# Crossbar DMA transposes for q, k and the attention output, wider score blocks and a fixed order on all engines, in a fused attention and MoE kernel

## The chip, the cores and the metric

The kernel runs on one core of a Trainium2 chip. The metric is the device time of one execution in microseconds (us), smaller is better. The profile is one execution of the same program. The engines are called PE (matmuls; PEld is its loading of weights, which overlaps PE), DVE (VectorE), ACT (ScalarE), POOL (GpSimd) and SP (SyncE, which here does nothing but issue DMAs). A "q" behind an engine's name (SPq) means its instruction queue.

## The reference

Eight batches of sliding-window attention with ALiBi bias come first; the result, 4608 tokens of 512 values, goes through one MoE-like block with a hard-swish. Cut to what matters:

```python
B, H, S, D = 8, 8, 576, 64
scores = q @ k.T / sqrt(D) + alibi_bias        # only where 0 <= i - j < 128
attn   = softmax(scores)                        # per head
x      = (attn @ v) -> [B * S, H * D] = [4608, 512]
h      = x @ w_in                               # w_in  [512, 2048]
g      = h * clip(h + 3, 0, 6) / 6
out    = g @ w_out                              # w_out [2048, 512]
```

## The kernel before

One PE stream holds everything. The attention goes by head pairs g (four pairs per batch, 32 in all); between its pieces the function `fill` puts MoE steps (four matmuls of 128x512 each), so that PE has work while the other engines do the softmax. There are 288 such steps, 144 up (`hps`) and 144 down (`ops`). An up step may be placed only when the tokens it needs have passed through attention.

The scores contract over the head dimension, so q and k are needed transposed. So does the first MoE matmul with the attention output. Before, PE makes all three transposes by matmuls with an identity, and DVE copies each result out of PSUM:

```python
def transposes(g):                       # q and k of one head pair
    b, hp = divmod(g, NP)
    for src, nm in ((qbuf[b % 2], "qT"), (kbuf[b % 2], "kT")):
        tp = ps_tp.tile([128, SP], BF16, tag="tp", name="tp")
        for j in range(NQ):              # NQ = 5
            nc.tensor.transpose(tp[:, ts(j, 128)], src[:, j, ts(hp, 128)], ident)
        t = qkt.tile([128, SP], BF16, tag=nm, name=nm)
        nc.vector.tensor_copy(out=t, in_=tp)
        st[g, nm] = t

def back(g):                             # attention output of one head pair
    avs = st[g, "avs"]
    tp = ps_tp.tile([128, SP], BF16, tag="tp", name="tp")
    for j in range(NQ):
        nc.tensor.transpose(tp[:, ts(j, 128)],
                            avs[:, j, :, :].rearrange("p e d -> p (e d)"), ident)
    nc.vector.tensor_copy(out=xT[:, hp, ds(b * S, S)], in_=tp[:, 0:S])
    done[0] = g + 1
```

The main loop fixes the order of PE alone; the other engines are ordered by the scheduler:

```python
with tc.manual_schedule(engines={mybir.EngineType.PE}):
    prepare(0)
    transposes(0)
    for g in range(G + 1):
        if g < G:
            scores_diag(g)
        if g + 1 < G:
            prepare(g + 1)               # casts; loads of the next batch
        fill(2)
        if g > 0:
            values(g - 1, (0, 1, 2))     # ends in the division result avs
        fill(1)
        if g > 0:
            values(g - 1, (3, 4))
        fill(1)
        if g < G:
            scores_off(g)
        fill(1)
        if g + 1 < G:
            transposes(g + 1)
        fill(1)
        if g > 0:
            back(g - 1)
        fill(2)
    fill(len(units))
```

The softmax here doesn't subtract the row's maximum and nothing guards it: scores larger than these inputs give would overflow.

Of the kernel before, what the change touches and what calls it, by code (L numbers as in the profile page):

```python
# [18 lines left out]
def kernel(  # L19
# [17 lines left out]
    NQ = 5  # L37
    LAST = S - 4 * 128
    SP = NQ * 128
    W = D + 1  # L40
    slopes = [2.0 ** (-8.0 * (h + 1) / H) for h in range(H)]
# [3 lines left out]
    n_nt = Ntok // NT  # L45

# [5 lines left out]
    bias3 = perm.tile([128, 1], FP32)  # L52
    rel_i = perm.tile([128, 1], INT32)
# [4 lines left out]
    loads = ctx.enter_context(tc.tile_pool(name="loads", bufs=4))  # L58
    held = ctx.enter_context(tc.tile_pool(name="held", bufs=1))
    qkt = ctx.enter_context(tc.tile_pool(name="qkt", bufs=3))  # L60
    ppool = ctx.enter_context(tc.tile_pool(name="ppool", bufs=3))
    small = ctx.enter_context(tc.tile_pool(name="small", bufs=4))
# [3 lines left out]
    ps_sc = ctx.enter_context(tc.tile_pool(name="ps_sc", bufs=1, space=bass.MemoryType.PSUM))  # L66
    ps_av = ctx.enter_context(tc.tile_pool(name="ps_av", bufs=1, space=bass.MemoryType.PSUM))
    ps_tp = ctx.enter_context(tc.tile_pool(name="ps_tp", bufs=2, space=bass.MemoryType.PSUM))
# [3 lines left out]
    qbuf = [held.tile([128, NQ, H * D], BF16, name=f"qbuf{i}") for i in range(2)]  # L72
    kbuf = [held.tile([128, NQ, H * D], BF16, name=f"kbuf{i}") for i in range(2)]
    vbuf = [held.tile([128, NQ, H, W], BF16, name=f"vbuf{i}") for i in range(2)]
    p4buf = [held.tile([128, 2, 128], BF16, name=f"p4buf{i}") for i in range(2)]

    srcs = (("qf", q), ("kf", k), ("vf", v))

    def new_loads():
        return {nm: loads.tile([128, NQ, H, D], FP32, tag="ld", name=nm) for nm, _ in srcs}  # L80

    def load_pair(got, b, hp):
        for nm, src in srcs:
            for h in (2 * hp, 2 * hp + 1):
                nc.sync.dma_start(out=got[nm][:, 0:4, h, :],
                                  in_=src[b, h, 0:512, :].rearrange("(t p) d -> p t d", p=128))
                nc.sync.dma_start(out=got[nm][:LAST, 4, h, :], in_=src[b, h, 512:S, :])  # L87

    def load_all(got, b):
        for nm, src in srcs:  # L90
            for j in range(NQ):
                n = min(128, S - j * 128)
                nc.sync.dma_start(
                    out=got[nm][:n, j, :, :],
                    in_=src[b, :, ds(j * 128, n), :].rearrange("h p d -> p h d"))

    got0 = new_loads()
    for hp in range(NP):
        load_pair(got0, 0, hp)

    make_identity(nc, ident)
    nc.vector.memset(bias3, 0.5)
    nc.gpsimd.iota(rel_i, pattern=[[0, 1]], base=0, channel_multiplier=1)
    nc.vector.tensor_copy(out=rel_f, in_=rel_i)
    for h in range(H):
        nc.vector.tensor_scalar(out=bias_d[:, h:h + 1], in0=rel_f, scalar1=-64.0,
                                scalar2=slopes[h], op0=ALU.add, op1=ALU.mult)
        nc.vector.tensor_scalar(out=bias_o[:, h:h + 1], in0=rel_f, scalar1=-192.0,
                                scalar2=slopes[h], op0=ALU.add, op1=ALU.mult)
    for i in range(2):  # L110
        nc.vector.memset(vbuf[i][:, :, :, D:W], 1.0)
        nc.vector.memset(vbuf[i][64:128, 4, :, 0:D], 0.0)
        nc.vector.memset(qbuf[i][64:128, 4, :], 0.0)
        nc.vector.memset(kbuf[i][64:128, 4, :], 0.0)
        nc.vector.memset(p4buf[i], 1.0)
# [13 lines left out]
    def cast_pair(got, b, hp, eng):  # L129
        for nm, dst in (("qf", qbuf[b % 2]), ("kf", kbuf[b % 2])):  # L130
            s = got[nm].rearrange("p j h d -> p j (h d)")
            eng.tensor_copy(out=dst[:, 0:4, ts(hp, 128)], in_=s[:, 0:4, ts(hp, 128)])  # L132
            eng.tensor_copy(out=dst[:LAST, 4, ts(hp, 128)], in_=s[:LAST, 4, ts(hp, 128)])
        hs = slice(2 * hp, 2 * hp + 2)
        vb = vbuf[b % 2]
        eng.tensor_copy(out=vb[:, 0:4, hs, 0:D], in_=got["vf"][:, 0:4, hs, :])
        eng.tensor_copy(out=vb[:LAST, 4, hs, 0:D], in_=got["vf"][:LAST, 4, hs, :])

    def cast_all(got, b):
        for nm, dst in (("qf", qbuf[b % 2]), ("kf", kbuf[b % 2])):  # L140
            s = got[nm].rearrange("p j h d -> p j (h d)")
            nc.gpsimd.tensor_copy(out=dst[:, 0:4, :], in_=s[:, 0:4, :])
            nc.gpsimd.tensor_copy(out=dst[:LAST, 4, :], in_=s[:LAST, 4, :])
        vb = vbuf[b % 2]
        nc.gpsimd.tensor_copy(out=vb[:, 0:4, :, 0:D].rearrange("p j h d -> p (j h) d"),
                              in_=got["vf"][:, 0:4, :, :].rearrange("p j h d -> p (j h) d"))
        nc.gpsimd.tensor_copy(out=vb[:LAST, 4, :, 0:D], in_=got["vf"][:LAST, 4, :, :])

    st = {}

    def transposes(g):
        b, hp = divmod(g, NP)
        for src, nm in ((qbuf[b % 2], "qT"), (kbuf[b % 2], "kT")):
            tp = ps_tp.tile([128, SP], BF16, tag="tp", name="tp")
            for j in range(NQ):
                nc.tensor.transpose(tp[:, ts(j, 128)], src[:, j, ts(hp, 128)], ident)  # L156
            t = qkt.tile([128, SP], BF16, tag=nm, name=nm)
            nc.vector.tensor_copy(out=t, in_=tp)  # L158
            st[g, nm] = t

    def scores_diag(g):
        b, hp = divmod(g, NP)
        qT, kT = st[g, "qT"], st[g, "kT"]
        sc = ps_sc.tile([128, 2, 512], FP32, tag="sc", name="sc")
        for j in range(4):
            for e in range(2):
                r = slice(e * D, (e + 1) * D)
                nc.tensor.matmul(sc[:, e, ts(j, 128)], lhsT=kT[r, ts(j, 128)],  # L168
                                 rhs=qT[r, ts(j, 128)], start=True, stop=True)
        pd = ppool.tile([128, 2, 4, 128], BF16, tag="pd", name="pd")  # L170
        for e in range(2):
            h = 2 * hp + e
            nc.scalar.activation(out=pd[:, e, :, :].rearrange("p j c -> p (j c)"),  # L173
                                 in_=sc[:, e, :], func=ACT.Exp,
                                 bias=bias_d[:, h:h + 1], scale=scale)
            nc.gpsimd.affine_select(out=pd[:, e, :, :], in_=pd[:, e, :, :],  # L176
                                    pattern=[[0, 4], [1, 128]], channel_multiplier=-1, base=0,
                                    compare_op=ALU.is_ge, fill=0.0)
        st[g, "pd"] = pd

    def scores_off(g):
        b, hp = divmod(g, NP)
        qT, kT = st[g, "qT"], st[g, "kT"]
        sc = ps_sc.tile([128, 2, 512], FP32, tag="sc", name="sc")
        for j in range(4):
            n = 128 if j < 3 else LAST
            for e in range(2):
                r = slice(e * D, (e + 1) * D)
                nc.tensor.matmul(sc[:, e, ds(j * 128, n)], lhsT=kT[r, ts(j, 128)],  # L189
                                 rhs=qT[r, ds((j + 1) * 128, n)], start=True, stop=True)  # L190
        for e in range(2):
            r = slice(e * D, (e + 1) * D)
            nc.tensor.matmul(sc[:, e, 448:512], lhsT=kT[r, 512:640],  # L193
                             rhs=qT[r, 512:576], start=True, stop=True)
        po = ppool.tile([128, 2, 4, 128], BF16, tag="po", name="po")
        p4 = p4buf[g % 2]
        for e in range(2):
            h = 2 * hp + e
            nc.scalar.activation(out=po[:, e, :, :].rearrange("p j c -> p (j c)"),  # L199
                                 in_=sc[:, e, :], func=ACT.Exp,  # L200
                                 bias=bias_o[:, h:h + 1], scale=scale)
            nc.scalar.activation(out=p4[:, e, 0:64], in_=sc[:, e, 448:512], func=ACT.Exp,  # L202
                                 bias=bias_d[:, h:h + 1], scale=scale)
            nc.gpsimd.affine_select(out=po[:, e, :, :], in_=po[:, e, :, :],  # L204
                                    pattern=[[0, 4], [-1, 128]], channel_multiplier=1, base=-1,
                                    compare_op=ALU.is_ge, fill=0.0)
        nc.gpsimd.affine_select(out=p4[:, :, 0:64], in_=p4[:, :, 0:64],
                                pattern=[[0, 2], [1, 64]], channel_multiplier=-1, base=0,
                                compare_op=ALU.is_ge, fill=0.0)
        st[g, "po"] = po  # L210
# [23 lines left out]

    def back(g):
        b, hp = divmod(g, NP)
        avs = st[g, "avs"]
# [61 lines left out]
    def prepare(g):  # L299
        b, hp = divmod(g, NP)  # L300
        if b == 0:
            cast_pair(got[0], 0, hp, nc.vector)
            if hp == 1:
                load_weights_in()
# [63 lines left out]
```

## Time and profile before

| | before |
|---|---|
| median of 3 runs | 419.31 us (417.61 to 419.33) |
| span of the profiled run | 417.7 us |
| PE busy | 81% |
| PE busy from 100 to 400 us | 93% |
| one head pair in the steady stretch | about 10 us |

The first page of the profile, kernel before: the busy time of each engine, then the span in 40 slices of 10.4 us (each digit is the busy share in tenths; PEclk is the granted PE clock in tenths), and the chain of waits that ended last ("issue" is time in which an engine waited for nothing that the profile shows).

```profile
PE 338.9 (81%) x2739; PEld 175.2 (42%) x2784; DVE 201.5 (48%) x438; ACT 198.5 (48%) x355; POOL 145.1 (35%) x217
...
PE   0141618878999899989998999899899999999985
...
PEclk9999999998999999999999999999999999999999
DMA  8989799997157989898470000001000000101011
...
PE 46%; DVE 15%; ACT 14%; issue 11%; DMA 8%; SPq 4%; POOL 1%; DVEq 0%; POOLq 0%; ACTq 0%
```

The PE row shows a start of about ten slices with many gaps, and then a stretch that is full. The windows view of the same kernel puts numbers on the two parts; its columns are the window, its length, the busy time and instruction count of PE, PEld, DVE, ACT and POOL, the granted clock, the DMA share and GB/s.

```profile
0.00:100.00 100.00, 47.72 (x492) 30.12 (x496) 44.10 (x125) 35.88 (x67) 45.15 (x69) 0.98 1.08 183
100.00:400.00 300.00, 279.55 (x2203) 140.21 (x2239) 156.06 (x312) 161.44 (x286) 99.90 (x148) 1.00 0.34 77
...
45.00:69.00 24.00, 11.61 (x130) 8.62 (x129) 8.94 (x24) 7.55 (x16) 12.00 (x17) 1.00 1.24 193
```

PE is busy 280 of 300 us after the start, so what PE has to do there sets the time. One pair of the steady stretch, in the timeline of PE (start, length, engine, line, operation, tiles; in brackets the idle time before it and what ended that):

```profile
143.17 0.40 PE L168 MATMUL sc<-qT,kT 64*128 64x128 bf16 x8
...
146.93 0.20 PE L222 MATMUL av<-vbuf,po 128*128 128x65 bf16 x1 [0.36 <-DVE avs L231]
...
149.34 0.44 PE L156 MATMUL tp<-ident,qbuf 128*128 128x128 bf16 x5
149.62 0.44 PE L156 MATMUL tp<-ident,kbuf 128*128 128x128 bf16 x5
...
150.77 0.44 PE L240 MATMUL tp<-ident,avs 128*128 128x128 bf16 x5
...
152.87 0.34 PE L168 MATMUL sc<-qT,kT 64*128 64x128 bf16 x6
```

The pair lasts from 143.17 to 152.87 us. Fifteen of its matmuls are transposes, 0.28 us for each group of five (149.34 to 149.62). Removing them, and the short wait for the division result `avs`, is what the change is after.

### The profile page before, as it was taken

Reading aid. Unit: us, or ns where it says so; the run is one execution under the profiler, and the core shown is the slowest. Engines: PE = TensorE matmul, PEld = TensorE weight load, DVE = VectorE, ACT = ScalarE, POOL = GpSimd, SP = SyncE. Lnnn points to the kernel's source line nnn. Section 1 sums busy time; section 2 is a strip of 40 time slices with the busy share of each in tenths; the row PEclk is TensorE's granted clock in tenths of the full one; section 3 lists DMA queues with packets and bytes.
Section 4 is the critical chain, followed back from the end, with each engine's and each line's share of the span. In section 5 each row is a group of like instructions: output and inputs, shape, how many; then the busy total and the mean of one; then the engine's idle time right before and its main releaser. Section 6 shows DMA issues by size and latency. Waiting matters only on the chain.

```text
span 417.7 us, 7115 instructions
## 1 busy us (share of the span) xinstructions
PE 338.9 (81%) x2739; PEld 175.2 (42%) x2784; DVE 201.5 (48%) x438; ACT 198.5 (48%) x355; POOL 145.1 (35%) x217
## 2 busy tenths in 40 slices
PE   0141618878999899989998999899899999999985
PEld 0021415445444444444454444444444444444432
DVE  3341614675455555555555555555555454344400
ACT  0240414675655565555565655556565534443400
POOL 3070464458657427342752374222222200000000
PEclk9999999998999999999999999999999999999999
DMA  8989799997157989898470000001000000101011
GB/s 134 195 148 199 151 198 197 209 201 135 49 132 166 179 176 166 161 186 152 116 163 25 27 26 27 27 27 39 32 31 27 27 25 30 48 25 52 25 70 55
DMA packets 122481, 42.40 MB, mean 101 GB/s; under 512 B 113744, under 2 KB 117840, under 8 KB 122448
## 3 DMA queue, kind: packets, MB, share of 16 engines
q1 hardware_dynamic: 118224, 37.76, 44.3%
q0 software_dynamic: 4224, 4.19, 6.2%
q8 instruction: 21, 0.34, 0.4%
q14 instruction: 12, 0.10, 0.1%
HBM read 36.70 MB, written 9.44 MB: 110 GB/s over the span
## 4 chain that ended last, share of the span: by engine, by line
PE 46%; DVE 15%; ACT 14%; issue 11%; DMA 8%; SPq 4%; POOL 1%; DVEq 0%; POOLq 0%; ACTq 0%
PE ops L267 22%; PE hps L253 13%; ACT r L257 8%; DMA vf<-in_v_dram 6%; DVE g L258 5%; DVE avs L231 4%; DVE osb L274 3%; ACT pd L173 3%; PE tp L156 2%; PE sc L168 2%; PE av L222 2%; PE sc L189 2%; ACT p4buf L202 2%; SPq L87 2%; DMA kf<-in_k_dram 2%
## 5 line engine op out<-in xcount | busy, mean ns | idle before, releaser
L258 DVE SCALAR_TENSOR_TENSOR g<-r,hps 128x512 bf16<-128x512 f32 x144 | 99.0, 687 | 117.0 <-ACT r L257 116.9
L253 PE MATMUL hps<-xT,w_in_sb 128*128 128x512 bf16 x535 | 144.4, 382 | 10.5 <-DVE xT L242 5.3
L267 PE MATMUL ops<-w_out_sb,g 128*128 128x512 bf16 x572 | 145.2, 379 | 5.6 <-DVE osb L274 3.1
L257 ACT ACTIVATE r<-hps,bias 128x512 f32<-128x512 f32 x144 | 99.2, 691 | 96.8 <-PE hps L253 93.9
L267 PEld LDWEIGHTS <-g 128*128 128x128 bf16 x576 | 53.6, 98 | 70.0 <-issue 15.1
L176 POOL TENSOR_SCALAR_AFFINE_SELECT pd<-pd 128x512 bf16<-128x512 bf16 x64 | 39.8, 644 | 96.9 <-ACT pd L173 96.9
L253 PEld LDWEIGHTS <-w_in_sb 128*128 128x128 bf16 x576 | 49.8, 98 | 49.9 <-issue 4.1
L204 POOL TENSOR_SCALAR_AFFINE_SELECT po<-po 128x512 bf16<-128x512 bf16 x64 | 40.4, 634 | 79.0 <-ACT po L199 75.7
L199 ACT ACTIVATE po<-sc,bias_o 128x512 bf16<-128x512 f32 x64 | 44.0, 687 | 39.3 <-PE sc L193 39.3
L173 ACT ACTIVATE pd<-sc,bias_d 128x512 bf16<-128x512 f32 x64 | 40.5, 683 | 43.1 <-PE sc L168 43.1
L222 PE MATMUL av<-vbuf,po 128*128 128x65 bf16 x256 | 26.1, 201 | 15.4 <-DVE avs L231 15.3
L158 DVE COPY qT<-tp 128x640 bf16<-128x640 bf16 x32 | 15.7, 492 | 35.9 <-PE tp L156 35.8
L156 PE MATMUL tp<-ident,kbuf 128*128 128x128 bf16 x160 | 16.4, 239 | 20.0 <-DVE kbuf L132 15.9
L231 DVE TENSOR_TENSOR avs<-av,rc 128x384 bf16<-128x384 f32 x64 | 31.4, 491 | 2.0
L156 PE MATMUL tp<-ident,qbuf 128*128 128x128 bf16 x160 | 16.2, 238 | 19.5 <-DVE qbuf L132 15.2
L222 PEld LDWEIGHTS <-po 128*128 128x128 bf16 x256 | 18.9, 102 | 29.3 <-DVE avs L231 29.0
L225 PE MATMUL av<-vbuf,pd 128*128 128x65 bf16 x256 | 25.0, 201 | 0.0
L156 PEld LDWEIGHTS <-qbuf 128*128 128x128 bf16 x160 | 12.1, 105 | 26.2 <-DVE qbuf L132 15.5
L225 PEld LDWEIGHTS <-pd 128*128 128x128 bf16 x256 | 20.0, 101 | 7.2 <-issue 0.8
L156 PEld LDWEIGHTS <-kbuf 128*128 128x128 bf16 x160 | 11.4, 106 | 21.6 <-DVE kbuf L132 16.9
L202 ACT ACTIVATE p4buf<-sc,bias_d 128x64 bf16<-128x64 f32 x64 | 20.2, 315 | 0.0
L274 DVE COPY osb<-ops 128x512 f32<-128x512 f32 x18 | 12.3, 685 | 16.0 <-PE ops L267 16.0
(46 smaller groups left out, 231.8 us busy)
## 6 DMA issues: line engine op xcount, KB each, us to landing
out_dram<-osb SPq DMA_DIRECT2D x36, 256.0 KB, 2.0
qf<-in_q_dram SPq DMA_DIRECT2D x28, 256.0 KB, 4.9
kf<-in_k_dram SPq DMA_DIRECT2D x28, 256.0 KB, 5.1
vf<-in_v_dram SPq DMA_DIRECT2D x28, 256.0 KB, 4.9
w_in_sb<-in_moe_w_in_dram POOLq DMA_DIRECT2D x4, 512.0 KB, 10.4
w_out_sb<-in_moe_w_out_dram POOLq DMA_DIRECT2D x4, 512.0 KB, 10.1
qf<-in_q_dram SPq DMA_DIRECT2D x15, 128.0 KB, 5.3
kf<-in_k_dram SPq DMA_DIRECT2D x15, 128.0 KB, 4.8
```

Of the source, the lines that this page charges most:

```text
L156: nc.tensor.transpose(tp[:, ts(j, 128)], src[:, j, ts(hp, 128)], ident)
L173: nc.scalar.activation(out=pd[:, e, :, :].rearrange("p j c -> p (j c)"), in_=sc[:, e, :], func=ACT.Exp, bias=bias_d[:, h:h + 1], scale=scale)
L176: nc.gpsimd.affine_select(out=pd[:, e, :, :], in_=pd[:, e, :, :], pattern=[[0, 4], [1, 128]], channel_multiplier=-1, base=0, compare_op=AL ...
L199: nc.scalar.activation(out=po[:, e, :, :].rearrange("p j c -> p (j c)"), in_=sc[:, e, :], func=ACT.Exp, bias=bias_o[:, h:h + 1], scale=scale)
L204: nc.gpsimd.affine_select(out=po[:, e, :, :], in_=po[:, e, :, :], pattern=[[0, 4], [-1, 128]], channel_multiplier=1, base=-1, compare_op=A ...
L222: nc.tensor.matmul(av[:, i, e, :], lhsT=po[:, e, qt - 1, :], rhs=vb[:, qt - 1, h, :], start=True, stop=False)
L225: nc.tensor.matmul(av[:, i, e, :], lhsT=d, rhs=vb[:, qt, h, :], start=(qt == 0), stop=True)
L231: nc.vector.tensor_tensor(out=st[g, "avs"][:, qts[0]:qts[0] + nq, :, :], in0=av[:, 0:nq, :, 0:D], in1=rc[:, 0:nq, :, :].to_broadcast([128, ...
L253: nc.tensor.matmul(hps, lhsT=w_in_sb[:, ks, ts(ms, 128)], rhs=xT[:, ks, ts(nt, NT)], start=(ks == 0), stop=(ks == n_ks - 1))
L257: nc.scalar.activation(out=r6, in_=hps, func=ACT.Relu, bias=bias3[:, 0:1], scale=1.0 / 6.0)
L258: nc.vector.scalar_tensor_tensor(out=gts[nt][:, ms, :], in0=r6, scalar=1.0, in1=hps, op0=ALU.min, op1=ALU.mult)
L267: nc.tensor.matmul(ops[nt, sub], lhsT=gts[nt][:, ms, ts(sub, 128)], rhs=w_out_sb[:, ms, :], start=(ms == 0), stop=(ms == n_ms - 1))
```

## The change

The intent: take the transposes of q, k and the output off PE (and their copies off DVE), for batches 2 to 7, and let the DMA crossbar do them from one queue, SP. The PSUM space that the transposes used goes to the scores: diagonal and off-diagonal scores of a pair are now made in one block, into two PSUM tiles (`scd`, `sco`) of 128x2x512 FP32. Batches 0 and 1 keep PE transposes, with new loads in longer runs, and run almost without MoE steps, so as to start soon. All five engines are put in program order.

The diff, cut to its core:

```diff
+    NB_PE = 2                           # batches that keep PE transposes
+    XBAR_X = True
-    loads = ctx.enter_context(tc.tile_pool(name="loads", bufs=4))
+    loads = ctx.enter_context(tc.tile_pool(name="loads", bufs=3))
-    ps_sc = ... tc.tile_pool(name="ps_sc", bufs=1, space=bass.MemoryType.PSUM)
+    ps_sc = ... tc.tile_pool(name="ps_sc", bufs=2, space=bass.MemoryType.PSUM)
-    ps_tp = ... tc.tile_pool(name="ps_tp", bufs=2, space=bass.MemoryType.PSUM)
...
+    def xbar(b, dst, src):              # q or k of one batch
+        for j in range(NQ):
+            n = min(128, S - j * 128)
+            nc.sync.dma_start_transpose(out=dst[:, :, ds(j * 128, n)], in_=src[:n, j, :])
...
     def back(g):
+        if XBAR_X and b >= NB_PE:
+            nc.sync.dma_start_transpose(
+                out=xT[:, hp, ds(b * S, 512)].rearrange("p (j c) -> p j c", j=4),
+                in_=avs[:, 0:4, :].rearrange("p j c -> p (j c)"))
+            nc.sync.dma_start_transpose(
+                out=xT[:, hp:hp + 1, ds(b * S + 512, LAST)], in_=avs[:LAST, 4, :])
+            return
...
+    def stage_next(g):                  # work for the next batch n, at each pair
+        b, hp = divmod(g, NP)
+        n = b + 1
...
+        if n >= NB_PE and n < B:
+            if hp == 0:
+                new_loads(n)
+                load_tokens(n, "q", q)  # five loads each, on SP
+                load_tokens(n, "k", k)
+                load_tokens(n, "v", v)
+            elif hp == 2:
+                cast_tokens(n, "q", qbuf)      # GpSimd
+                xbar(n, qTb[n % 2], qbuf)      # five transposes, on SP
+                cast_tokens(n, "k", kbuf)
+            elif hp == 3:
+                xbar(n, kTb[n % 2], kbuf)      # five transposes, on SP
+                cast_v(n, None, nc.gpsimd)
...
+    def segment(lo, hi, fills):         # one pair g per turn
...
+            if g < hi:
+                scores(g)
+            fill(f[0])
...
+            if g > lo:
+                values(g - 1, (0, 1, 2))
...
+            if g > lo:
+                values(g - 1, (3, 4))
...
+            if g > lo:
+                back(g - 1)
...
+            if g < hi:
+                stage_next(g)
+            fill(f[6])
...
-    with tc.manual_schedule(engines={mybir.EngineType.PE}):
+    with tc.manual_schedule(engines=every):     # PE, DVE, ACT, POOL, SP
```

## The prediction

> **What bounds the kernel now.** The page gives PE 81% busy over 417.7 us. The windows view splits it: from 100 to 400 us PE is busy 93 to 95%, but only 47.7 of the first 100 us. So there is a slow start, and a PE-bound rest. The chain of waits agrees: 46% PE, and early DMA pieces (12.7 us until the first v lands).
>
> In the steady stretch (timeline, 143.17 to 152.87 us) one head pair takes 9.7 us; over 22 pairs (104.8 to 324.3 us) the mean is 10.0. It holds eight MoE steps of 0.864 us (6.9), 15 transposes at about 0.056 us (0.84), 36 score and value matmuls at 0.03 to 0.04 us (1.3), and waits: 0.36 us for the division result `avs`, and 0.93 us for `xT` near one batch boundary.
>
> **What changes.**
> 1. Batches 2-7 lose the 15 PE transposes per pair, three DVE copies (0.49+0.48+0.45 us), and most of the `avs` wait, since two MoE steps now stand between the value blocks. PE's floor per pair becomes 6.9+1.3 = 8.2 us against 10.0; at 8.4 that saves 24 x 1.6 = 38 us, all on the critical path. ACT (5.4 us per pair by my sum) and DVE (4.1) stay below.
> 2. New on SP's queue, per batch: 18 transposes (10 for q and k, 8 for the output), beside 15 loads and 4 stores. The loads take about 17 us of issue (three groups of five, 4.4 to 6.8 us each, at about 200 GB/s). No run shows a transpose yet. The Trainium skill ("DMA: Bandwidth & Descriptors", "Latency and other measured facts") gives 261 GB/s for a non-contiguous one: estimated 0.5 us per 131 KB; I guess 1 us of issue. SP then has 17+18+2 = 37 us per batch, against PE's 33.5.
> 3. The next batch's k transposes stand on SP behind a pair's output transposes, which wait for its `avs`; PE has only four MoE steps (3.5 us) before the scores that need them. Seven issues plus landing is 6 to 10 us: I expect a PE stall of 3 to 6 us at each of six boundaries, about 27 us. It eats much of point 1. Pair 12 also starves for MoE steps (output marked ready one pair later), about 3 us.
> 4. Start: batches 0 and 1 load q and k as 1536-byte runs, batch 0 on two queues, with far fewer issues (before: 48, the last at 46 us; first `hps` matmul at 69 us). They run attention with few fills at 4.5 to 5 us a pair. I estimate that batch 2 starts near 75 us with 14 MoE steps done; before, the 17th came at about 102 us. That gains about 25 us, though batch 2 loads and w_out compete around 50 to 80 us.
> 5. Tail: split last store, about 1 us.
>
> **Sum.** 75 + 274 x 0.864 (237) + 25 x 1.3 (33) + stalls 30 + tail 4 = 379; I say 380 us, range 362 to 406. Faster by over 2%: 0.85; within 2%: 0.09; slower: 0.06.
>
> **Right or wrong would show as:** transposes and their copies gone in batches 2-7; pair period near 8.3 us inside a batch; PE idle before the first scores of batches 2-7, released by a DMA of `kTb`; SP issue nearly full; first `hps` matmul before 45 us; final pure-MoE stretch about 63 us.
>
> **What would break it:** a transpose costing over 2 us of SP or DMA time (SP then sets the pace, 45 us or more per batch); GpSimd blocked on load landing, holding the masks; stores stuck behind 15 loads and filling the two output buffers; or, upward, transposes so cheap that the boundary stalls vanish (about 355 us).

## More of the kernel before

The clock stays near its top (0.98 in the first 100 us, then 1.00).

Between 45 and 69 us the DMA queues of this kernel were full.

## The result, and the profile after

| | before | after |
|---|---|---|
| median, same rounds | 419.32 us (4 runs, 417.61 to 421.77) | 484.36 us (4 runs, 483.95 to 486.32) |
| ratio after / before | | 1.1555 (95% interval 1.1489 to 1.1621) |
| PE busy | 338.9 us | 337.6 us |
| mean granted clock | 0.996 | 0.858 |

The change made the kernel 15.6% slower, not 9% faster. All outputs are right. Ratios here and below are the mean time of one kernel's fast runs over that of the other's fast runs of the same rounds, so they are not quite the ratio of the medians quoted.

The first page of the profile, kernel after (the slices are now 12.1 us long):

```profile
PE 337.6 (70%) x2405; PEld 167.9 (35%) x2440; DVE 173.1 (36%) x357; ACT 201.4 (42%) x365; POOL 145.1 (30%) x219
...
PE   1568563006993789059863996299638999999986
...
PEclk9999767556998799659985998679876999999999
DMA  9998019968714199447954396419841112011011
...
PE 52%; SPq 19%; DMA 9%; DVE 5%; ACT 5%; issue 4%; POOL 4%; POOLq 0%; DVEq 0%
```

PE has 334 instructions fewer and is hardly less busy, as part of its work ran at a lower clock: the PE row now has a hole at about 75 to 105 us and then one hole per batch, and PEclk falls in each. SP's queue, 4% of the chain before, is now 19% of it. The windows view of the kernel after, columns as before:

```profile
0.00:100.00 100.00, 45.31 (x454) 28.22 (x457) 42.05 (x108) 38.34 (x72) 41.33 (x67) 0.82 0.83 150
100.00:400.00 300.00, 214.66 (x1586) 104.44 (x1611) 100.34 (x201) 133.22 (x248) 103.73 (x152) 0.83 0.57 114
...
45.00:69.00 24.00, 15.29 (x128) 8.40 (x126) 13.27 (x27) 12.32 (x22) 7.46 (x12) 0.72 0.01 3
```

The loss is in the middle: 215 busy us of 300, where the kernel before had 280. The view of waits says for what PE waits (engine, tile, line, releaser: total us, times, longest us):

```profile
PE scd L200 <- DMA kTb<-kbuf: 80.4, 24, 26.0
```

Of the 80 us, about 29 come before batch 2 (26.0 in one wait) and the rest before the first scores of batches 3 to 7. Inside a batch the change does what it was made for. In the timeline of PE, kernel after:

```profile
178.41 0.40 PE L200 MATMUL scd<-qTb,kTb 64*128 64x128 bf16 x8
...
186.52 0.40 PE L200 MATMUL scd<-qTb,kTb 64*128 64x128 bf16 x8
...
206.67 0.29 PE L200 MATMUL scd<-qTb,kTb 64*128 64x128 bf16 x2 [11.97 <-DMA kTb<-kbuf]
...
214.22 1.91 PE L307 MATMUL ops<-w_out_sb,g 128*128 128x512 bf16 x4
...
217.94 1.03 PE L307 MATMUL ops<-w_out_sb,g 128*128 128x512 bf16 x4
```

A pair takes 8.11 us (178.41 to 186.52), as against 9.7 before. Then, at the boundary to batch 4, PE stands for 12 us, and the first matmul groups after that run at half speed: 1.91 us for four, where 1.03 is usual. Why k's transposes came so late is told by SP's own timeline. This is one whole round of it, from the loads of batch 4 to those of batch 5:

```profile
171.68 4.22 SPq L110 DMA_DIRECT2D ld_q<-in_q_dram  x5
175.95 6.88 SPq L110 DMA_DIRECT2D ld_k<-in_k_dram  x5
182.93 5.54 SPq L110 DMA_DIRECT2D ld_v<-in_v_dram  x5
188.56 1.26 SPq L272 DMA_TRANSPOSE xT<-avs  x1
189.87 1.22 SPq L275 DMA_TRANSPOSE xT<-avs  x1
...
194.42 6.42 SPq L162 DMA_TRANSPOSE qTb<-qbuf  x5
...
204.15 7.04 SPq L162 DMA_TRANSPOSE kTb<-kbuf  x5
211.29 0.53 SPq L322 DMA_DIRECT2D out_dram<-osb  x1
220.12 1.20 SPq L272 DMA_TRANSPOSE xT<-avs  x1
221.37 1.21 SPq L275 DMA_TRANSPOSE xT<-avs  x1
222.64 2.11 SPq L110 DMA_DIRECT2D ld_q<-in_q_dram  x3
```

SP is busy without a gap worth naming from 171.68 to 211.82 us: 40.1 us. Then it stands still for 8.3 us until 220.12, waiting for the `avs` of batch 3's last pair, and after 2.5 us of output transposes the next round begins. A round takes 51 us (loads of batches 4, 5, 6 and 7 start at 171.68, 222.64, 274.14 and 325.51 us: 51.3 on average).

So SP waits for PE while PE has just waited for SP. That is **theory 1, the loop**. The last pair's values stand on PE behind the first scores of the next batch. Those scores need k's transposes. The last pair's output transposes need those values. And all of the following loads, and so the following transposes, stand on SP behind these output transposes. SP's 42.6 us (40.1 and the 2.5 of output transposes) and the 8.3 us in which it stands still do not overlap; they add. The 8.3 us are PE's part: the landing of the last k transpose, scores and values, most of it at half clock.

For the start, the same two timelines: no load is issued on SP between 41.8 and 69.6 us. The view of waits of SP's queue gives the reason:

```profile
SPq L110 <- POOL pr L172: 23.8, 1, 23.8
```

Batch 2's loads need the three load buffers, and those are held until GpSimd has cast the last k of batch 1. The window from 45 to 69 us shown above has 3 GB/s in it, where the kernel before moved 193. The first scores of batch 2 run at 106.4 us; the prediction had said 75. In PE's timeline:

```profile
106.44 0.29 PE L200 MATMUL scd<-qTb,kTb 64*128 64x128 bf16 x2 [25.99 <-DMA kTb<-kbuf]
```

The rivals that I set against the loop:

- **Theory 2, the clock.** The clock dropped to 0.858 on average. If that is the loss rather than its companion, a PE kept warm through the stalls should recover it.
- **Theory 3, DMA bandwidth.** The transposes' bytes (the queues moved 53.0 MB instead of 42.4) make everything on the queues late. Then the order of issue would not matter.
- **Theory 4, the crossbar itself is too dear.** Then every version with crossbar transposes would lose to one without.

### The profile page after: what moved, and what is told of

It is laid out like the page before. It is cut to its first block, busy times and chain, and to the rows that moved or that the text cites. A ratio compares the mean times of both kernels' runs of the same rounds, so it can differ in the third digit from the quotient of the medians.

```text
span 484.6 us, 6565 instructions
## 1 busy us (share of the span) xinstructions
PE 337.6 (70%) x2405; PEld 167.9 (35%) x2440; DVE 173.1 (36%) x357; ACT 201.4 (42%) x365; POOL 145.1 (30%) x219
## 4 chain that ended last, share of the span: by engine, by line
PE 52%; SPq 19%; DMA 9%; DVE 5%; ACT 5%; issue 4%; POOL 4%; POOLq 0%; DVEq 0%
PE hps L290 22%; PE ops L307 22%; SPq L162 8%; SPq L110 7%; DMA kTb<-kbuf 3%; DMA out_dram<-osb 3%; ACT r L294 3%; PE av L256 2%; DMA ld_q<-in_q_dram 2%; DVE g L295 2%; PE av L253 2%; ACT po L230 2%; SPq L272 2%; POOL vbuf L146 2%; SPq L275 1%
## 5 line engine op out<-in xcount | busy, mean ns | idle before, releaser
L290 PE MATMUL hps<-xT,w_in_sb 128*128 128x512 bf16 x551 | 158.8, 406 | 8.1 <-DVE g L295 2.4
L307 PE MATMUL ops<-w_out_sb,g 128*128 128x512 bf16 x566 | 150.4, 393 | 16.9 <-DVE osb L321 15.8
L200 PE MATMUL scd<-qTb,kTb 64*128 64x128 bf16 x256 | 18.5, 247 | 80.4 <-DMA kTb<-kbuf 80.4
L220 ACT ACTIVATE pd<-scd,bias_d 128x512 bf16<-128x512 f32 x64 | 40.6, 684 | 14.8 <-PE scd L200 12.1
L230 ACT ACTIVATE po<-sco,bias_o 128x512 bf16<-128x512 f32 x64 | 44.1, 689 | 0.0
L200 PEld LDWEIGHTS <-kTb 64*128 64x128 bf16 x256 | 9.1, 102 | 95.4 <-DMA kTb<-kbuf 86.3
L256 PEld LDWEIGHTS <-pd 128*128 128x128 bf16 x256 | 22.6, 110 | 12.1 <-issue 4.8
L261 DVE RECIPROCAL rc<-av 128x6 f32<-128x6 f32 x64 | 11.8, 184 | 37.9 <-PE av L256 37.8
L185 PE MATMUL tp<-ident,pr 96*128 96x96 bf16 x96 | 9.1, 260 | 22.8 <-DVE pr L172 16.3
L233 ACT ACTIVATE p4buf<-sco,bias_d 128x64 bf16<-128x64 f32 x64 | 20.8, 324 | 0.0
L319 ACT COPY osb<-ops 128x512 f32<-128x512 f32 x18 | 10.5, 585 | 17.5 <-PE ops L307 17.5
```

The costliest lines, as they stand in the source:

```text
L220: nc.scalar.activation(out=pd[:, e, :, :].rearrange("p j c -> p (j c)"), in_=sc[:, e, :], func=ACT.Exp, bias=bias_d[:, h:h + 1], scale=scale)
L230: nc.scalar.activation(out=po[:, e, :, :].rearrange("p j c -> p (j c)"), in_=sc[:, e, :], func=ACT.Exp, bias=bias_o[:, h:h + 1], scale=scale)
L256: nc.tensor.matmul(av[:, i, e, :], lhsT=d, rhs=vb[:, qt, h, :], start=(qt == 0), stop=True)
L290: nc.tensor.matmul(hps, lhsT=w_in_sb[:, ks, ts(ms, 128)], rhs=xT[:, ks, ts(nt, NT)], start=(ks == 0), stop=(ks == n_ks - 1))
L307: nc.tensor.matmul(ops[nt, sub], lhsT=gts[nt][:, ms, ts(sub, 128)], rhs=w_out_sb[:, ms, :], start=(ms == 0), stop=(ms == n_ms - 1))
```

## The experiments

They ran in three sets, each on one chip, together with the kernel before. Its medians were 419.93, 419.04 and 421.62 us (7 runs each). e1 to e7 each start from the kernel after. e8 to e10 build on each other, and the diffs of e9 and e10 are shown against the experiment before. All diffs are cut to their core.

### e1: the attention output back on PE

```diff
-    XBAR_X = True
+    XBAR_X = False
```

> The attention output goes back to PE transposes, q and k of batches 2-7 stay on the crossbar. Theory 1 (SP's fixed order closes a loop: k transposes, first scores of the batch, division result of the batch before, its output transposes, 15 loads, q and k transposes; 51.5 us a batch): the loop is cut, SP has 17+13+2 = 32 us a batch, the batch takes about 36 us, total 400 to 415 us; the wait for kTb falls from 80 to about 35 us. Theory 2 (the transposes or loads are limited by the DMA engines' bandwidth): a third of the transposed bytes goes, total about 460 us. Theory 3 (the restructured order itself is slow, crossbar or not): little change, 475 us or more.

Measured: 459.84 us (2 runs), ratio 1.0954. The round became shorter, 51.3 to 44.2 us (loads at 168.89, 212.96, 257.16 and 301.42), and the wait for `kTb` fell from 80.4 to 51.2 us. But I had expected 400 to 415, and that was missed. The reason can be read in SP's timeline of e1:

```profile
195.76 6.43 SPq L162 DMA_TRANSPOSE kTb<-kbuf  x5
212.58 0.33 SPq L322 DMA_DIRECT2D out_dram<-osb  x1
212.96 5.32 SPq L110 DMA_DIRECT2D ld_q<-in_q_dram  x5
```

The loop was not cut; it closes through another item. `avs` no longer goes through SP, but a store of `osb` stands on SP between the k transposes and the next loads, and PE makes that output only after the first scores of the batch. SP issues for 33.3 us (168.89 to 202.19), then stands still for 10.4 us until DVE has written `osb` (212.54 us); the next two rounds have the same pause (10.5 and 10.6 us). So the two engines still take turns: 33.3 + 10.8 is the round of 44.1 us. No run took this store out of the way alone. A pair now takes 9.08 us instead of 8.11; beside the transposes themselves, PE waits 0.53 us in most pairs for `hps`, which now shares its two PSUM buffers with them. At the boundary the k tiles arrive about 1.3 us apart (PE waits about 1.05 us for each), because their issue begins less than 2 us before PE comes to the scores that need them.

### e2: no crossbar at all, in the new order

```diff
-    NB_PE = 2
+    NB_PE = 8
...
-        if n == 1 and hp == 2:
-            new_loads(1)
+        if (n == 1 and hp == 2) or (1 < n < B and hp == 1):
+            new_loads(n)
             for i in range(NP):
-                load_pair(1, i, nc.sync)
+                load_pair(n, i, nc.sync)
```

> All batches use PE transposes, q, k and v of all batches load as in batch 1 of the changed kernel; the fixed order, one block of scores and the MoE slots stay. Theory 1: a pair takes about 9.1 us on PE, batch 2 starts near 75 us, total 370 to 390 us, faster than the kernel before. Theory 3 (restructured order itself slow): 420 us or more.

Measured: 439.81 us (4 runs), ratio 1.0494. The 370 to 390 expected was a clear miss. Without any crossbar transpose this version still loses 20 us to the kernel before, so by subtraction about 45 of the 65 us lost come with the crossbar in this order. That is a rough split, as e2 also loads and casts batches 2 to 7 in another way than the kernel after. Two places in the trace of e2 show where time goes: its SP waits 47.2 us in two waits for load buffers, and batch 2 begins at 95.0 us; and its round is 42.3 us instead of about 40, with PE waiting 14.8 us for `hps` and another 7.1 us for transposes because both now take turns in the same two PSUM buffers. This is read from the trace; giving the transposes other buffers again was not tried.

### e3: the five transposes of q, and of k, as one each

The rows of q and k are laid out so that one instruction of 128x2560 does what five of 128x512 did; the scores read the blocks at their new places.

```diff
-        for j in range(NQ):
-            n = min(128, S - j * 128)
-            nc.sync.dma_start_transpose(out=dst[:, :, ds(j * 128, n)], in_=src[:n, j, :])
+        nc.sync.dma_start_transpose(
+            out=dst.rearrange("p h s -> p (h s)").rearrange("p (n c) -> p n c", c=128),
+            in_=src.rearrange("p j c -> p (j c)"))
```

> The five q transposes of a batch become one of 128x2560, and the five of k likewise; same bytes. If the SP cost is per instruction (about 1.25 us whatever the size): SP saves 8 x 1.25 = 10 us a batch, the loop shrinks to about 41 us a batch and the start by about 10 us, total about 425 us. If the cost follows the bytes or tiles: 6.4 us for each, total unchanged near 484 us. A DMA bandwidth limit (theory 2) also says unchanged.

Measured: 454.7 us (2 runs), ratio 1.0832, between the two answers that I had foreseen. The timeline of SP in e3:

```profile
187.35 3.09 SPq L162 DMA_TRANSPOSE qTb<-qbuf  x1
...
193.74 3.04 SPq L162 DMA_TRANSPOSE kTb<-kbuf  x1
```

One large transpose takes 3.0 to 3.1 us of SP here (up to 3.8 in the whole run) where five small ones took 6.4 to 7.0 in the round above (up to 7.2). The cost is thus neither per instruction nor per byte alone. What matters for the theory is the round: it fell from 51.3 to 44.8 us, by 6.5, and SP's work in a round fell by (6.42 + 7.04) - (3.09 + 3.04) = 7.3 us in the two rounds shown, or 6.7 with the usual 6.4 for five. SP time saved comes off the round almost one for one, as the loop says. If SP ran beside PE with time to spare, it would have saved less: at most the k part, 3.4 to 4.0 us, or nothing.

### e4: the next q and k loads right behind the k transposes

```diff
             if hp == 0:
-                new_loads(n)
-                load_tokens(n, "q", q)
-                load_tokens(n, "k", k)
+                if n == NB_PE:
+                    new_loads(n)
+                    load_tokens(n, "q", q)
+                    load_tokens(n, "k", k)
                 load_tokens(n, "v", v)
...
                 cast_v(n, None, nc.gpsimd)
+                if n + 1 < B:
+                    new_loads(n + 1)
+                    load_tokens(n + 1, "q", q)
+                    load_tokens(n + 1, "k", k)
```

> Only SP's order changes: the q and k loads of the batch after next stand right behind the k transposes, ahead of the last pair's output transposes; the v loads stay. Same bytes, same number of issues. Theory 1: 11 of the 17 us of loads leave the loop and fill the 8 us in which SP waits for the division result; 51.5 becomes about 43 us a batch, total 440 to 450 us. Theory 2 (bandwidth) and theory 3: no change, about 484 us.

Measured: 471.77 us (2 runs), ratio 1.1239; I had expected 440 to 450. The round is 47.9 us, 3.4 less. Ten loads now fall into SP's idle 8 us, but they also stand before the last pair's output transposes, and PE now waits 11.2 us in all for `xT`, where the kernel after had 2.2. The view of waits of e4:

```profile
PE scd L200 <- DMA kTb<-kbuf: 68.9, 23, 24.9
```

It is a half answer: moving work into the gap helps, but the k transposes are still issued at the last moment, and the wait for `kTb` is still 68.9 us in all.

### e5: keep PE warm through the boundary

Before the first scores of batches 3 to 7, PE gets matmuls whose result is overwritten.

```diff
+        if b > NB_PE and hp == 0:
+            for _ in range(WARM if b > NB_PE + 1 else WARM // 2):    # WARM = 56
+                nc.tensor.matmul(scd[:, 0, :], lhsT=w_in_sb[:, 0, 0:128],
+                                 rhs=w_in_sb[:, 0, 0:512], start=True, stop=True)
```

> Dummy matmuls (28 of 128x512 before the first scores of batch 3, 56 before those of batches 4 to 7, overwritten by the scores) keep PE busy while it waits for kTb; nothing else changes. Theory 1 (the time is set by SP's chain, the low clock is its consequence and costs only the few us of half-speed work after each landing, about 3 us a batch): total 465 to 480 us, the batch stays near 48 to 51 us, although the granted clock rises to about 0.93. Rival: the low clock itself is the cause; 0.858 of 484.6 us are 69 us lost, nearly all to be won back: about 420 us.

Measured: 480.68 us (2 runs), ratio 1.1465 (1.1376 to 1.1555); the gain of some 4 us is not clear of noise, as this interval overlaps that of the kernel after. The mean clock rose from 0.858 to 0.921, but not where it was meant to. The timeline of PE in e5, at the boundary to batch 4:

```profile
197.16 12.25 PE L200 MATMUL scd<-w_in_sb 128*128 128x512 bf16 x56
...
214.74 1.89 PE L295 MATMUL hps<-xT,w_in_sb 128*128 128x512 bf16 x4
```

The extra matmuls fill the long wait, but after them PE again waits about 1 us for each tile of k, and the first groups of real work still take 1.89 to 1.91 us. So e5 did not keep PE warm through the boundary, and it does not test theory 2 as planned. What bounds theory 2 is the trace of the kernel after: from the last of the delayed scores (211.42 us) to the first group at full speed (217.94 us) it takes 6.5 us for what takes about 3.5 us inside a batch. That makes an estimate of 3 us for each boundary, some 15 us of the 65 at the five of them, and it comes only after a stall. The low clock is thus a companion that makes the loop dearer, not what starts it; e7 below returns 51 us by order alone.

The Trainium skill ("TensorE: Matmul & The Clock Gate", Part 1: The HAM clock gate) says that an idle window of about 3.4 us halves the clock and that a similar time of work restores it. The trace of the kernel after agrees in kind: the groups of four take 1.91 us after the 12 us stall and 1.03 again at 217.94 us, some 6 us after PE had resumed without gaps. The restoring thus took longer here than the page's window, and the measured time is the one to use.

### e6: batch 2 loaded by casting DMAs from GpSimd's queue, early

```diff
+        if g == 2:
+            cast_load(2, "q", q, qbuf)     # five DMAs each, f32 to bf16
+            cast_load(2, "k", k, kbuf)
+        if g == 4:
+            cast_load(2, "v", v, vbuf[0])
+        if n == NB_PE:                     # no SP loads, no casts
+            if hp == 2:
+                xbar(n, qTb[n % 2], qbuf)
+            elif hp == 3:
+                xbar(n, kTb[n % 2], kbuf)
-        if n >= NB_PE and n < B:
+        elif n > NB_PE and n < B:
```

> Only batch 2's way in changes: its q, k and v come by casting DMAs from GpSimd's queue straight into the bf16 buffers, issued during batch 0, so they wait for no load buffer and need no cast. If the idle stretch of 26 us before batch 2 is due to the load buffers being held until batch 1's last casts (SP waits 23.8 us there): first scores of batch 2 at about 80 us, total about 457 us. If it is DMA bandwidth or w_out's 4 MB: first scores still at 95 us or later, total 470 us or more.

Measured: 465.65 us (2 runs), ratio 1.1107, a gain of 19 us. The wait of 26 us before batch 2 is gone, and with it SP's wait for load buffers, its longest piece. (e6 also takes SP's loads and the casts off batch 2's way, and does not tell these apart.) But batch 2's first scores ran at 92.6 us, not at the 80 expected. GpSimd was held from 33.6 to 42.8 us by the k loads, and batch 0's last masks stood behind them; batch 1 began at 66.4 us instead of 55.5, and these 10.9 us are most of the 12.6 missed. The jam had moved to another queue.

### e7: the same work on SP, in another order

This is the test of theory 1 against theory 3. For batches 3 to 7 the same loads, casts and transposes are issued, with the same bytes. But q is transposed at pair 0 of the batch before, k at pair 1, v is cast at pair 2, and each is followed at once by the load of the batch after, into the buffer just freed. The k transposes then have two pairs of slack.

```diff
-        if n >= NB_PE and n < B:
+        if n == NB_PE:
...
                 cast_v(n, None, nc.gpsimd)
+                for nm, s in (("q", q), ("k", k), ("v", v)):
+                    new_load(n + 1, nm)
+                    load_tokens(n + 1, nm, s)
+        elif NB_PE < n < B and hp < 3:
+            nm, s = (("q", q), ("k", k), ("v", v))[hp]
+            if nm == "v":
+                cast_v(n, None, nc.gpsimd)
+            else:
+                dst, t = (qbuf, qTb) if nm == "q" else (kbuf, kTb)
+                cast_tokens(n, nm, dst)
+                xbar(n, t[n % 2], dst)
+            if n + 1 < B:
+                new_load(n + 1, nm)
+                load_tokens(n + 1, nm, s)
```

> For batches 3 to 7 only the order changes: casts and transposes of q, k and the cast of v stand at pairs 0, 1, 2 of the batch before, each followed by the load of the same tensor for the batch after. Same instructions, same bytes. Theory 1: no transpose is needed within 8 us of its issue any more, the loop is open and the batch takes SP's own work, 17+22.5+2 = about 41.5 us (PE needs 33); total about 435 us, kTb waits (after batch 2) near zero, PE then waits for xT or for output buffers. If DMA bandwidth or the instruction order of the other engines set the pace: little change from 484 us.

Measured: 432.94 us (2 runs), ratio 1.0327, against about 435 expected. The order alone is worth 51 of the 65 us lost. The view of waits of e7:

```profile
PE scd L203 <- DMA kTb<-kbuf: 28.8, 4, 25.8
PE ops L310 <- ACT osb L322: 23.2, 4, 6.7
```

The wait for `kTb` is now batch 2's alone; 52 us of it have gone. Theory 3 falls: the same bytes in the same queues, and the boundaries are free. (Bandwidth is not without effect: while loads are issued, as from 171 to 189 us in the kernel after, the DMA share is 1.04 at 183 GB/s, and the five loads of q take 4.2 us of issue at 171.68 us but 13.9 us at 69.61, while `w_out` comes in. So part of SP's time for loads is waiting for the queues.) e7 changes two links at once, the early issue of the transposes and the place of the loads. e4 had changed only the second, for q and k, and gained 13 us; so the larger part seems to lie in the early issue, though no run changed that alone. The round is 41.0 us (q transposes at 169.16, 209.84, 251.43 and 292.03), and SP is issuing for nearly all of it. SP has become what sets the pace, and it shows as PE waiting for an output buffer: the stores stand behind transposes and loads in the same queue.

### e8: everything together

e8 is e7 with e3's merged q and k, with the two output transposes of a pair merged into one, and with e6's start, where batch 2's q and k are now transposed one pair earlier.

```diff
-    xT = perm.tile([128, n_ks, Ntok], BF16)
+    xT = perm.tile([128, n_ks, Ntok + 64], BF16)
...
-                out=xT[:, hp, ds(b * S, 512)].rearrange("p (j c) -> p j c", j=4),
-                in_=avs[:, 0:4, :].rearrange("p j c -> p (j c)"))
-            nc.sync.dma_start_transpose(
-                out=xT[:, hp:hp + 1, ds(b * S + 512, LAST)], in_=avs[:LAST, 4, :])
+                out=xT[:, hp, ds(b * S, SP)].rearrange("p (j c) -> p j c", j=NQ),
+                in_=avs.rearrange("p j c -> p (j c)"))
```

> The reorder, one crossbar transpose each for q, k (128x2560) and for a pair's output (128x640), and batch 2's early casting loads together. Theory 1: SP has 17+6.2+5+2 = 30 us a batch, less than PE's 33; batch 2 starts at about 78 us, pair period about 8.3 us, total 350 to 365 us, faster than both kernels. If something else than SP's queue limits the crossbar version: 390 us or more.

Measured: 382.54 us (4 runs), ratio 0.9124 (0.9073 to 0.9176): faster than both kernels, though not the 350 to 365 expected. The windows view of e8, one stretch of the steady part:

```profile
150.00:200.00 50.00, 50.00 (x427) 25.26 (x427) 25.86 (x53) 34.93 (x65) 27.91 (x40) 1.00 1.04 188
```

PE is busy 50.00 of 50 us, at full clock, with the crossbar in use, and a steady round is 32.5 us, four pairs of 8.1. Theory 4 falls: this version beats both versions without a crossbar transpose, the kernel before and e2. (A version without the crossbar but with this start was not tried.) What missed is the start again:

```profile
PE av L272 <- POOL pd L239: 9.2, 2, 8.9
```

Batch 0's last masks (`pd`) still stand behind GpSimd's casting loads; batch 1 begins at 65.7 us, and batch 2 only at 91.8 us, where 78 had been expected.

### e9: the casting loads one pair later

```diff
-        if g == 2:
+        if g == 3:
             cast_load(2, "q", q, qbuf)
             cast_load(2, "k", k, kbuf)
```

> As the version with everything together, but batch 2's casting loads of q and k are issued one pair later, when GpSimd has no masks of batch 0 left to make. In that version GpSimd stood blocked behind them (8.9 us in which PE waited for a mask near 43 us). If that wait is the cause of the late batch 1: the first scores of batch 1 come about 10 us earlier (56 instead of 65.7 us), total about 373 us. If the time was only hidden by another wait (weights or loads of batch 1): 380 us or more.

Measured: 372.43 us (4 runs, 371.7 to 373.6), ratio 0.8851 (0.8802 to 0.8899), against 373 expected. This is the fastest version found: 11.5% below the kernel before. Batch 1 begins at 55.25 us, and batch 2 at 81.35:

```profile
81.35 0.40 PE L216 MATMUL scd<-qTb,kTb 64*128 64x128 bf16 x8
```

SP's timeline in e9, for the round that starts at 165.79 us:

```profile
165.79 3.09 SPq L171 DMA_TRANSPOSE qTb<-qbuf  x1
...
176.42 3.58 SPq L171 DMA_TRANSPOSE kTb<-kbuf  x1
...
186.67 5.45 SPq L119 DMA_DIRECT2D ld_v<-in_v_dram  x5
...
198.25 3.07 SPq L171 DMA_TRANSPOSE qTb<-qbuf  x1
```

The k transposes are issued 12.8 us before their scores (189.17 us on PE), and the next round begins 32.46 us later. SP now waits for PE, not the other way round. What is left of the start (batch 1's first three pairs take 7.1, 9.0 and 5.3 us) was not pursued.

### e10: the crossbar from batch 1 on

```diff
-    NB_PE = 2
+    NB_PE = 1
...
-        if g == 3:
-            cast_load(2, "q", q, qbuf)     # ... and so on for batch 2
+        if g == 3:
+            cast_load(1, "q", q, qbuf)
+            cast_load(1, "k", k, kbuf)
+            cast_load(1, "v", v, vbuf[1])
+            xbar(1, qTb[1], qbuf)
+            xbar(1, kTb[1], kbuf)
+        if g == NP:                        # 15 SP loads of batch 2
...
```

> Batch 1 goes the crossbar way too, by casting loads of q, k and v on GpSimd's queue at the end of batch 0; batch 2 comes by SP loads. Batch 1 then has no PE transposes, no copies and no casts: about 5 us a pair instead of 7 to 9. Theory 1: SP still has room, batch 2 starts near 80 us, total 355 to 368 us. If the loads of batch 1 and 2 (with the weights some 15 MB at 200 GB/s) are the limit of the start instead: 370 us or more.

Measured: 388.69 us (4 runs), ratio 0.9237, the second of the two outcomes. The view of waits and one line of the windows view of e10:

```profile
PE scd L216 <- DMA kTb<-kbuf: 28.0, 2, 21.1
```

```profile
80.00:100.00 20.00, 1.03 (x18) 0.95 (x20) 0.00 (x0) 0.00 (x0) 2.86 (x4) 0.50 1.18 207
```

PE waits for k twice, 6.9 us before batch 1 and 21.1 before batch 2, and at that time the DMA queues move 207 GB/s, somewhat above the 193 that the kernel before moved in its full stretch. So loads seem to be the limit here, as the early batches and both weight matrices compete; this is read from the trace, and no run separates it from the order of issue. Bandwidth, wrong as the reason of the boundaries, may be real at the start.

## Why the prediction was wrong, point by point

- **"PE's floor per pair becomes ... 8.2 us": right.** A pair takes 8.11 us inside a batch, and the kernels e8 and e9 hold four pairs in 32.5 us in their steady rounds.
- **"SP then has 17+18+2 = 37 us per batch": nearly right.** In the round shown, SP's issues from the loads to the last output transposes took 40.1 + 2.5 = 42.6 us. Loads took 16.6, the stores as guessed. The transposes took about 1.2 to 1.4 us each instead of 1, 23.2 for 18. The size of a transpose hardly mattered: 1.21 us for 64x128, 1.22 to 1.26 for 128x512. The bandwidth of 261 GB/s that the prediction took from the Trainium skill ("DMA: Bandwidth & Descriptors", "Latency and other measured facts") was not what set the pace: 131 KB per 1.25 us of issue is 105 GB/s.
- **"I expect a PE stall of 3 to 6 us at each of six boundaries, about 27 us": this step failed.** It named the right order (k transposes behind the output transposes, which wait for `avs`), the right tile and the right wait, but priced it as a single short delay between two engines that otherwise ran side by side, SP at 37 us and PE at 33.5. The order makes them take turns: SP's 42.6 us, then 8.3 us in which SP waits for PE. The round was 51.3 us, where the prediction implied 4 x 8.4 + 4.5 = 38. Five boundaries at 13 us too much are about 66 us. e7 showed this by removing the loop with the same instructions and bytes: 51 us came back. e3 showed it by the one-for-one gain, and e1 by a round that is again the sum of two turns.
- **"I estimate that batch 2 starts near 75 us": this step failed too.** It was 106.4 us. The estimate followed loads and PE pairs, and did not ask when the load buffers come free. With three instead of four, batch 2's loads waited 23.8 us for batch 1's last cast, with the DMA queues idle; afterwards they met `w_out` and took 27.6 us instead of 17. Batch 1's pairs took 7.1, 7.8, 5.3 and 4.7 us, not 4.5 to 5, so that PE came to batch 2's scores at 80.4 us; the other 26.0 of the 31 us are the wait. The first `hps` matmul, before 45 us as predicted (37.7), did not help, as there were few MoE steps to do by then. e6 removed the wait; e9 began batch 2 at 81.4 us, 6 later than the estimate.
- **The sum.** 31 us from the start and 66 from the boundaries explain 97 of the 104 us between 380 and 484. The remaining 7 were not broken down.
- **What the prediction listed as able to break it.** Transposes took 1.2 us in the median (a few of the output's reached 2.3 to 2.5), so this was not what broke it. GpSimd did block on load landing (one wait of 13.3 us for `ld_q`, during the start). Stores did get stuck behind SP's other work: PE waited for an output buffer, 15.8 us in nine waits, the longest of 3.9 us. The case that did break it, a loop through two engines in fixed order, was not on the list.

The Trainium skill ("DMA: Bandwidth & Descriptors", "Issuing engines are not separate DMA queues") says of the time to initiate a DMA on a sequencer that it "is usually small relative to the DMA itself". For the small transposes it was not small: 1.2 us of issue, where the median from issue to landing is 2.4 us. SP is at such issues, 18 of them, for 23.2 of the 51 us of a round, and e3 took 30 us off the time by merging ten of them into two. The same skill ("Advanced Engine Details and Errata", X-Bar Transpose (TRN2)) says that transposes by DMA are as fast as regular ones. In this trace the five transposes of q (590 KB) take 6.42 us of issue, and five loads (1.18 MB) take 4.22 to 6.88, so by time of issue that holds at best for the large ones: 655 KB in 3.05 us.

These points stay open: what in SP makes a small transpose cost 1.2 us whatever its size; how much of e2's loss in the steady part is really the sharing of PSUM buffers; how the 51 us of e7 split between the early issue and the place of the loads; what a PE that is really warm at the boundary would save; and how far the start could be shortened beyond e9.

## What to carry to other kernels

When work moves from a busy engine to a queue in program order, do not compare the totals of the two engines; follow one item around and ask whether what it waits for stands behind something that waits for it. If the path closes over two engines, their times add, and issuing the consumer's input one or two stages earlier, with the next load right behind it, was worth more here (51 us, e7) than making the steps cheaper (30 us, e3). Look for every item on the path: with the output transposes gone, a single store closed it again (e1). And ask when each buffer comes free before believing that an early load will be early.

## What the Trainium skill lacked or had wrong

- "DMA: Bandwidth & Descriptors" gives a bandwidth for DMA transposes, but no issue time, named as one of trn2, for small ones between SBUF tiles. The runs show medians of 1.21 us for 64x128 and 1.23 us for 128x512, and 3.0 to 3.8 us for 128x2560, with a median landing of 2.4 us for the small and 4.9 to 5.1 us for the large ones. A planner needs the first number.
- "DMA: Bandwidth & Descriptors", Issuing engines are not separate DMA queues, calls the time to initiate a DMA usually small relative to the DMA. For small transposes it was half of it here: 1.2 us of issue, 2.4 us to landing.
- "Advanced Engine Details and Errata", X-Bar Transpose (TRN2), calls transposes as fast as regular DMAs. By time of issue, five loads went at 171 to 280 GB/s; a transpose came near that only with 655 KB at once (215 GB/s), and with 131 KB the pace was 105 GB/s.
- No page that I read says that casting loads issued from GpSimd can hold up its other work: with eight of q and k issued, the next issue waited 3.5 us for an earlier one to land (e6), and PE waited up to 8.9 us for masks behind the loads (e8).
